# First loads in halves on two queues, filler matmuls on zeros and a re-searched order in a fused sparse-attention and FFN kernel

## The chip, the cores and the metric

One Trainium2 chip, one core of it. The metric is the device time of one execution in microseconds (us). Engines are named as in the profile: PE (TensorE), PEld (its weight loads), DVE (VectorE), ACT (ScalarE), POOL (GpSimd), SP (SyncE); a "q" behind a name, as in SPq or ACTq, is the sequencer of that engine, which issues DMAs.

## What is computed

Two stages in one kernel. The first is attention with 4 batches of 8 heads, 768 positions and head size 64, in which each query keeps six key chunks of 32 positions. The chunks are chosen by an upper bound made of the minimum and the maximum of the keys of a chunk:

```
k_min, k_max = min and max of k over each chunk of 32
ub = sum(max(q*k_min, q*k_max), -1)          # causal over chunks
top_chunks = argsort(ub)[..., -6:]
scores = where(selected and causal, q @ k.T / 8, -1e9)
attn = softmax(scores) @ v
```

The second is a gated FFN over the 3072 rows of 512 values that the attention gives: `xn = x / rms(x) * rms_g`, then `(silu(xn @ w_gate) * (xn @ w_val)) @ w_out` with a hidden size of 1536.

## The kernel before

**Tiling.** Two heads make a pair, so there are 16 pairs, four to a batch. A pair goes through these steps (the names are those of the planner's steps and of the tiles; the lines are those of the kernel before):

- *load* (L486): q and k of the pair, 768 rows, one DMA for each head and tensor into `qnat` and `knat` (192 KB each). The loads of pair 0 put their first head on SP's queue and their second on ACT's; all others are on SP's.
- *turn* (L499): PE transposes, in groups of three 128x128 blocks, two groups for q and two for k; ACT or DVE copies each group out of PSUM (`kt`, `qt`, L315 on ACT and L319 on DVE).
- *kmx, kmn, dif* (L523, L525, L534): maximum, minimum and their difference for each chunk, into `ku`; *relu* (L560): max(q, 0), into `rt`.
- *ub* (L578): 24 matmuls, twelve on `qt` and twelve on `rt`, give the bounds; they are copied out (`ubs`), transposed back (*up*, L602), masked (`ubm`, L610), and twelve MAX8 (L623) find the sixth largest bound of each query; *pick* (L631, L636) makes the selection `selq`, which PE transposes (`st`, L647) and which ACT and DVE put into the lower or upper half of `qs`.
- *sc, exp, av* (L712, L718, L729, L748): per head six groups of scores, an exponential on ACT for each group, and the product with v.

When the four pairs of a batch are through, *norm* scales and transposes the rows (`xs`, `tp`, `xT`) and *ffn* runs on halves of 384 rows: twelve times gate (`gp`, L864), tanh (`sg`, L871), `tg` (L877), value (`vp`, L885), `hh` (L893), then the output product `po` (L905), its copy `osb` and a DMA out.

**What sets the order.** Nothing is reordered by a compiler. Every step is given to `Order.add` with the engines that may run it, an assumed duration, a rank and the steps it depends on. `Order.run` plays these steps forward: whenever an engine is free, it takes the ready step of lowest rank whose buffers are free, and so fixes the engine and the place of each step. The emitted program is that list, and each engine then executes its own part strictly in that order. A rank is the sum of a due time of the pair or FFN half (`TIMES`: a = prepare, l = load, s = scores, n = norm, f = FFN, w = weights) and an offset for the kind of step (`RANK`, one set for batch 0 and one for the rest). The planner doubles the duration of PE steps that start before `COLD` = 10.0 us.

Constants come first: the identity matrix on POOL, zeros in `ku` and `selq` on DVE, `first` on ACT (a one-column Exp, which also brings the activation table in; L354), the mask helpers `e_all` and `cmf` on POOL. `ke0` copies `e_all` into the first key tile on DVE (L391, L392); `ke` does it for the other two by DMA on SP.

A DMA is issued with one of eight completion semaphores of its kind; where one of them is used again, the issuing engine waits until the earlier DMA on it has landed. In the program before, ACT's second load (the second head of k of pair 0) waits in this way for a first load of q.

Of the kernel before, what the change touches and what calls it, by code (L numbers as in the profile page):

```python
# [24 lines left out]

RANK = (
    dict(
        av=-17.99, dif=13.38, eps=15.18, exp=27.56, kC=-0.16, kE=17.53, kT=-23.78, kload=11.87,
        kmn=22.63, kmx=-12.26, max=-61.12, qC=54.11, qE=9.45, qT=-26.18, qload=3.56,
        relu=19.97, root=46.9, sc=-0.2, sel=-44.38, selC=-65.79, selT=-14.62, sq=17.6, tp=7.31,  # L30
        tpE=23.87, ub=-8.14, ubE=18.31, ubm=-7.93, up=-18.76, vload=-10.11, xb=16.97, xs=25.31,
    ),
    dict(
        av=-15.37, dif=-18.4, eps=-17.61, exp=10.72, gate=-5.25, hh=-22.22, kC=13.17, kE=-4.98,
        kT=-1.03, kload=0.17, kmn=-41.84, kmx=7.41, mask=-29.68, max=20.31, out=-9.4, po=2.14,
        poE=-2.1, qC=3.39, qE=-3.84, qT=-9.81, qload=-3.16, relu=-0.35, root=5.16, sc=-14.52,
        sel=-54.35, selC=-24.54, selT=7.81, sq=37.75, tanh=-21.52, tg=-0.17, tp=-45.38,
        tpE=12.9, ub=-13.71, ubE=24.1, ubm=13.82, up=-10.31, val=1.94, vload=19.85, xb=5.4,
        xs=11.14,
    ),  # L40
)

TIMES = dict(
    pace0=1.79, pace1=0.05, pacen=0.06, step=0.1, w=-2.85, w0=-2.54, w1=11.0, w2=43.12,
    w3=21.59,
)
for p, x in enumerate((
    13.52, 22.61, 22.24, 36.48, 50.85, 112.1, 73.87, -93.04, 37.77, 179.84, 214.26, 206.91,
    226.56, 220.49, 246.48, 309.33,
)):  # L50
    TIMES[f"a{p}"] = x
for p, x in enumerate((
    -126.16, -42.1, -31.16, -25.49, -5.8, -2.4, 25.7, 37.05, 124.03, 155.87, 181.98, 170.69,
    131.44, 202.23, 282.06, 292.24,
)):
    TIMES[f"l{p}"] = x
for p, x in enumerate((
    -21.19, 10.14, 25.24, 47.31, 25.73, 45.99, 41.69, 141.19, 75.77, 129.26, 185.37, 166.25,
    277.81, 251.34, 143.95, 194.34,
)):  # L60
    TIMES[f"s{p}.0"] = x
for p, x in enumerate((
    101.79,
), 3):
    TIMES[f"s{p}.3"] = x
for i, x in enumerate((
    -27.88, 91.19, 93.6, 105.43, 90.44, 106.14, 282.0, 341.37,
)):
    TIMES[f"n{i // 2}.{i % 2}"] = x
for i, x in enumerate((  # L70
    50.8, 120.12, 121.42, 191.74, 229.9, 291.93, 266.48, 339.66,
)):
    TIMES[f"f{i // 2}.{i % 2}"] = x
for i, x in enumerate((
    2.53, 0.58, 0.91, 2.16, 0.75, 2.5, 0.51, 0.73,
)):
    TIMES[f"pacef{i // 2}.{i % 2}"] = x

class Buf:
# [138 lines left out]
def kernel(  # L224
# [84 lines left out]
    def pe(n):  # L309
        return 0.003 + n / 2400.0  # L310

    def evict(e, out_, in_, scale=None):
        if e == "ACT":
            if scale is None:
                nc.scalar.activation(out=out_, in_=in_, func=ACT.Copy)  # L315
# [20 lines left out]
    e_all = const.tile([D, S], BF16, name="e_all")  # L336
# [10 lines left out]
    def make_ident(e):  # L347
# [6 lines left out]
    c_act = add("first", "ACT", 1.6, -99, lambda e: nc.scalar.activation(  # L354
        out=first[:], in_=ident_f[:, 0:1], func=ACT.Exp), [c_id])
# [31 lines left out]
    c_ke = [None] * NB  # L387
    for i in range(NB):
        if i == 0:
            c_ke[i] = add("ke0", "DVE", 1.05, -50, lambda e: (  # L390
                nc.vector.tensor_copy(KE[0][0][D:2 * D, :], e_all[:]),  # L391
                nc.vector.tensor_copy(KE[0][1][0:D, :], e_all[:])), [c_e])  # L392
        else:
            c_ke[i] = add("ke", "SP", 1.0, -25, lambda e, i=i: (
                nc.sync.dma_start(out=KE[i][0][D:2 * D, :], in_=e_all[:]),
                nc.sync.dma_start(out=KE[i][1][0:D, :], in_=e_all[:])), [c_e], load=200000)

# [73 lines left out]
    def prep(c, i0, nb, at, lr):  # L471
# [7 lines left out]
        for w, src in (("k", k), ("q", q)):  # L479
            nat[w], big[w] = Buf("nat"), Buf("qt")  # L480

            def load(e, w=w, src=src):
                t = tile_of(nat[w], [P, NT, 2, D], FP32, w + "nat")
                for hl in range(2):
                    eng = nc.scalar if p == 0 and i0 == 0 and hl else nc.sync
                    eng.dma_start(out=t[:, 0:nb, hl, :], in_=src[b, h0 + hl, cols].rearrange(  # L486
                        "(t p) d -> p t d", p=P))

            ld = add(w + "load", "SP", 1.1, rank(lr, b, w + "load"), load, opens=[nat[w]],
                     load=n * 512)  # L490

            evs = []
            for j0 in range(0, nb, 3):
                bank = Buf("ps", "prep")

                def turn(e, w=w, j0=j0, bank=bank):
                    t = tile_of(bank, [P, 3 * P], FP32, "p" + w)
                    for j in range(3):
                        nc.tensor.transpose(  # L499
                            t[:, j * P:(j + 1) * P],  # L500
                            nat[w].tile[:, j0 + j].rearrange("p h d -> p (h d)"), ident_f[:])

                tr = add(w + "T", "PE", 0.33, rank(at, b, w + "T", j0, "step"), turn, [ld, c_id],
                         opens=[bank], uses=[nat[w]])
# [11 lines left out]

        mx = Buf("small")

        def red(e, which):
            view = big["k"].tile[:, 0:n].rearrange("p (c t) -> p c t", t=CH)  # L520
            if which == 0:
                t = tile_of(mx, [P, NCH], FP32, "kmx")
                nc.vector.tensor_reduce(out=t[:, 0:c1 - c0], in_=view, axis=AXX, op=ALU.max)  # L523
            else:
                nc.vector.tensor_reduce(out=KU[c.ku.slot][:, 0, c0:c1], in_=view, axis=AXX,  # L525
                                        op=ALU.min)

        r0 = add("kmx", "DVE", 0.06 + n * 0.00106, rank(at, b, "kmx"), lambda e: red(e, 0), done["k"],
                 opens=[mx], uses=[big["k"]])
        r1 = add("kmn", "DVE", 0.06 + n * 0.00106, rank(at, b, "kmn"), lambda e: red(e, 1),  # L530
                 done["k"] + c_ku, opens=[c.ku], uses=[big["k"]])
# [6 lines left out]
        df = add("dif", "", {"DVE": 0.12, "POOL": 0.2}, rank(at, b, "dif"), diff, [r0, r1],  # L538
                 uses=[mx, c.ku], port=True)
        c.dif[i0] = df  # L540

# [426 lines left out]
```

## Time and profile before

| | |
|---|---|
| device time, median of 3 runs | 328.62 us (328.37 to 329.08) |
| the profiled execution: span from first to last instruction | 461.2 us |
| mean granted TensorE clock in the profiled execution | 0.663 |
| granted clock, first 12 us / from 13 us on | 1.00 / 0.65 |

The profiled execution is the only one with a trace. No total time of its own is given beside the span, and its span is longer than the whole of an unprofiled run, since TensorE had a lower clock in it. Times in the trace's rows are us from the start of the span. A row of the timeline gives the start, the duration, the engine, the line, the operation, out<-in, and how many instructions were merged.

### The profile page before, as it was taken

The numbers are of one execution on the slowest core, as the hardware profiler recorded it, in microseconds if no ns is written. First come the engines' busy times: TensorE is split into PE (matmuls) and PEld (weight loads), VectorE is DVE, ScalarE is ACT, GpSimd is POOL, SyncE is SP. The second block draws the span as 40 slices with busy tenths as digits, with TensorE's granted clock in tenths as the row PEclk, the third lists the DMA queues.
The fourth block names the chain that finished last, engine by engine and source line by source line (L and its number), as shares of the span: only waits on it lengthen the run. The fifth ranks groups of instructions, "written<-read, shape, count | busy, mean of one in ns | idle before, by whom it ended". The sixth has DMA issues, their size and how long they took to land.

```text
span 461.2 us, 7853 instructions
## 1 busy us (share of the span) xinstructions
PE 446.6 (97%) x2978; PEld 253.4 (55%) x2996; DVE 246.5 (53%) x663; ACT 214.3 (46%) x448; POOL 118.0 (26%) x172
## 2 busy tenths in 40 slices
PE   3999999999999999999999999999999999999996
PEld 2677754665666555435666664654565644534442
DVE  2977776665465735404767564367046465603520
ACT  3777772463556643114656684630473634123201
POOL 7755342314442420002552453200110110000000
PEclk9666666666666666666666666666666666666666
DMA  9999769248848250003430203100100000011002
GB/s 186 210 207 143 104 105 100 41 47 53 185 89 134 18 112 9 0 30 105 111 36 1 18 2 46 41 1 1 47 24 0 2 0 1 1 63 52 0 0 91
DMA packets 82645, 27.89 MB, mean 60 GB/s; under 512 B 75568, under 2 KB 79408, under 8 KB 82608
## 3 DMA queue, kind: packets, MB, share of 16 engines
q1 hardware_dynamic: 52528, 19.14, 17.9%
q0 software_dynamic: 28512, 7.87, 17.3%
q10 hardware_dynamic: 1568, 0.39, 0.5%
q8 instruction: 23, 0.38, 0.3%
q14 instruction: 14, 0.11, 0.1%
HBM read 28.57 MB, written 6.29 MB: 76 GB/s over the span
## 4 chain that ended last, share of the span: by engine, by line
PE 96%; DMA 2%; ACT 1%; issue 1%; ACTq 0%
PE vp L885 20%; PE gp L864 20%; PE po L905 20%; PE sc L712 12%; PE av L748 6%; PE ub L578 5%; PE pk L499 3%; PE pq L499 3%; PE tp L830 2%; PE up L602 2%; PE st L647 2%; DMA knat<-in_k_dram 1%; PE sc L718 1%; DMA qnat<-in_q_dram 1%; ACT pt L729 0%
## 5 line engine op out<-in xcount | busy, mean ns | idle before, releaser
L885 PE MATMUL vp<-xT,wv 128*128 128x384 bf16 x384 | 107.5, 430 | 0.0
L864 PE MATMUL gp<-xT,wg 128*128 128x384 bf16 x384 | 107.3, 430 | 0.0
L729 ACT ACTIVATE pt<-sc 128x512 bf16<-128x512 f32 x192 | 91.1, 551 | 20.5 <-PE sc L712 16.6
L905 PE MATMUL po<-wo,hh 128*128 128x512 bf16 x274 | 97.8, 513 | 1.9 <-issue 0.8
L871 ACT ACTIVATE sg<-gp 128x384 bf16<-128x384 f32 x96 | 47.1, 491 | 88.9 <-PE gp L864 78.9
L877 DVE SCALAR_TENSOR_TENSOR tg<-sg,gp 128x384 bf16<-128x384 bf16 x96 | 52.5, 550 | 52.2 <-ACT sg L871 51.4
L893 DVE TENSOR_TENSOR hh<-vp,tg 128x384 bf16<-128x384 f32 x96 | 53.1, 555 | 38.1 <-PE vp L885 37.9
L712 PE MATMUL sc<-qs,ke 89*128 89x128 bf16 (+5 forms) x416 | 72.1, 309 | 0.4 <-PE sc L712 0.2
L885 PEld LDWEIGHTS <-wv 128*128 128x128 bf16 x384 | 45.3, 120 | 43.7 <-issue 3.4
L864 PEld LDWEIGHTS <-wg 128*128 128x128 bf16 x384 | 45.1, 120 | 41.4 <-issue 2.5
L905 PEld LDWEIGHTS <-hh 128*128 128x128 bf16 x288 | 33.5, 120 | 46.8 <-issue 43.8
L735 POOL TENSOR_SCALAR_AFFINE_SELECT pt<-pt 128x512 bf16<-128x512 bf16 (+1 forms) x48 | 24.8, 532 | 102.1 <-ACT pt L729 100.5
L748 PEld LDWEIGHTS <-pt 128*128 128x128 bf16 x672 | 39.1, 111 | 16.5 <-issue 8.2
L712 PEld LDWEIGHTS <-ke 89*128 89x128 bf16 (+1 forms) x420 | 38.2, 116 | 16.0 <-issue 8.6
L748 PE MATMUL av<-vx,pt 128*128 128x65 bf16 x672 | 45.2, 217 | 0.3 <-ACT pt L729 0.2
L317 ACT ACTIVATE osb<-po 128x512 f32<-128x512 f32 x23 | 13.7, 597 | 64.5 <-PE po L905 64.5
L319 POOL CAST ke<-kt 64x768 bf16<-64x768 f32 x31 | 26.1, 843 | 61.0 <-ACT kt L315 57.5
L319 POOL CAST qs<-qt 64x768 bf16<-64x768 f32 x31 | 29.0, 936 | 49.1 <-ACT qt L315 32.5
L499 PE MATMUL pq<-ident_f,qnat 128*128 128x128 f32 x96 | 20.4, 358 | 5.2 <-DMA qnat<-in_q_dram 5.2
L499 PE MATMUL pk<-ident_f,knat 128*128 128x128 f32 x96 | 21.7, 354 | 2.7 <-DMA knat<-in_k_dram 2.5
L525 DVE TENSOR_REDUCE ku<-kt 128x24 f32<-128x768 f32 x16 | 15.1, 945 | 12.7 <-ACT kt L315 12.6
L820 DVE SCALAR_TENSOR_TENSOR xs<-xb,ri,gains 128x512 bf16<-128x512 bf16 x24 | 17.3, 758 | 7.8 <-PE tp L830 5.2
(70 smaller groups left out, 366.7 us busy)
## 6 DMA issues: line engine op xcount, KB each, us to landing
out_dram<-osb SPq DMA_DIRECT2D x24, 256.0 KB, 2.0
qnat<-in_q_dram SPq DMA_DIRECT2D x31, 192.0 KB, 4.8
knat<-in_k_dram SPq DMA_DIRECT2D x31, 192.0 KB, 4.5
vx<-in_v_dram POOLq DMA_DIRECT2D x16, 192.0 KB, 4.7
wv<-in_moe_w_val_dram POOLq DMA_DIRECT2D x2, 768.0 KB, 7.9
wg<-in_moe_w_gate_dram POOLq DMA_DIRECT2D x2, 768.0 KB, 7.0
wo<-in_moe_w_out_dram POOLq DMA_DIRECT2D x2, 768.0 KB, 7.6
ke<-e_all SPq DMA_DIRECT2D x4, 96.0 KB, 3.5
```

The source lines that it names most:

```text
L319: engine[e].tensor_copy(out_, in_)
L499: nc.tensor.transpose(t[:, j * P:(j + 1) * P], nat[w].tile[:, j0 + j].rearrange("p h d -> p (h d)"), ident_f[:])
L712: nc.tensor.matmul(t[:, x:x + m, :].rearrange("p a b -> p (a b)"), ke[kk, kb * P:(kb + 1) * P], qs[kk, q0 * P:(q0 + m) * P], start=not tri ...
L729: nc.scalar.activation(out=t[:, 0:nn, :], in_=sc.tile[:, 0:nn, :], func=ACT.Exp, scale=SCALE)
L735: nc.gpsimd.affine_select(out=pt.tile[:, 0:nd, :], in_=pt.tile[:, 0:nd, :], compare_op=ALU.is_ge, fill=0.0, base=0, pattern=[[0, nd], [1, ...
L748: nc.tensor.matmul(av.tile[:, qi - i0, :], pt.tile[:, x, :], VX[c.v.slot][:, hl * NT + kb, :], start=(begin and m == 0), stop=(left[0] == ...
L864: nc.tensor.matmul(t[:], wg[:, g, hs], XT[b].tile[:, g, cols], start=(g == 0), stop=(g == NP - 1))
L871: nc.scalar.activation(out=t[:], in_=gp.tile[:], func=ACT.Tanh, scale=0.5)
L877: nc.vector.scalar_tensor_tensor(out=t[:], in0=sg.tile[:], scalar=1.0, in1=gp.tile[:], op0=ALU.add, op1=ALU.mult)
L885: nc.tensor.matmul(t[:], wv[:, g, hs], XT[b].tile[:, g, cols], start=(g == 0), stop=(g == NP - 1))
L893: nc.vector.tensor_tensor(out=t[:], in0=vp.tile[:], in1=tg.tile[:], op=ALU.mult)
L905: nc.tensor.matmul(po.tile[:], hhs[ht].tile[:, th * P:(th + 1) * P], wo[:, ht, :], start=(ht == 0), stop=(ht == NHT - 1))
```

## The change

Four things are changed.

1. Pair 0 loads k before q, each tensor in two halves of 384 rows, so eight DMAs of 96 KB in place of four of 192 KB, at ranks -200 to -197, ahead of all other loads. The first head stays on SP's queue, the second on ACT's. Each group of transposes waits for its own half, and pair 0's chunk maxima and minima are taken half by half.
2. `busy`: 48 matmuls of 128x512 on a tile of zeros, at ranks from 1000 up, so that the planner puts one wherever it sees PE free and a PSUM bank open. `COLD` is 4.5 in place of 10.0.
3. `ke0` may now run on ACT or DVE, its rank and that of `ke` are searched, and the assumed duration of `first` is 3.2 in place of 1.6.
4. All numbers of `RANK` and `TIMES` are new.

The core of the diff:

```diff
-    COLD = 10.0
+    COLD = 4.5
...
+    BUSY = 48
...
-    c_act = add("first", "ACT", 1.6, -99, lambda e: nc.scalar.activation(
+    c_act = add("first", "ACT", 3.2, -99, lambda e: nc.scalar.activation(
         out=first[:], in_=ident_f[:, 0:1], func=ACT.Exp), [c_id])
+    zeros = const.tile([P, 4 * P], BF16, name="zeros")
+    c_zero = add("zeros", "DVE", 0.2, -101, lambda e: nc.vector.memset(zeros[:], 0.0))
+
+    def busy(bank):
+        def go(e):
+            t = tile_of(bank, [P, 4 * P], FP32, "busy")
+            nc.tensor.matmul(t[:], zeros[:, 0:P], zeros[:], start=True, stop=True)
+        return go
+
+    for i in range(BUSY):
+        bank = Buf("ps")
+        add("busy", "PE", pe(4 * P), 1000.0 + i, busy(bank), [c_zero], opens=[bank])
...
-            c_ke[i] = add("ke0", "DVE", 1.05, -50, lambda e: (
+            c_ke[i] = add("ke0", "", {"DVE": 1.05, "ACT": 1.4}, {"ke0": 1.0}, lambda e: (
...
                 for hl in range(2):
-                    eng = nc.scalar if p == 0 and i0 == 0 and hl else nc.sync
+                    eng = nc.scalar if p == 0 and hl else nc.sync
...
-            ld = add(w + "load", "SP", 1.1, rank(lr, b, w + "load"), load, opens=[nat[w]],
-                     load=n * 512)
+            if p == 0:
+                ld = [add(w + "load", "SP", 0.55, -200 + 2 * (w == "q") + r0 / 3,
+                          lambda e, load=load, r0=r0: load(e, r0=r0, rn=3), opens=[nat[w]],
+                          load=3 * P * 512) for r0 in range(0, nb, 3)]
...
+        step = 3 if p == 0 else nb
+        for x0 in range(0, nb, step):
+            after = done["k"][x0 // 3:(x0 + step) // 3]
+            lead = {"": -10.0} if p == 0 and x0 == 0 else {}
```

Since the planner decides the places, the diff alone doesn't show the order; the two programs' lists of instructions do. At the start they read as follows.

- ACT, changed: the two halves of k (second head), the table load, `first`, then the two halves of q (second head). The first of these two waits for the completion semaphore of the second half of k, of one head, and the second for that of the other head. Then come two `kt` copies, two copies of `e_all` into `ke`, one cast of `kt`, one `qt` copy and so on.
- SP, changed: the two halves of k, the two of q, both heads of q of pair 1, both heads of k of pair 1 (waiting for the first half of k of pair 0), four `ke` DMAs, q and k of pair 2.
- PE, changed, up to the first scores (n x busy stands for n filler matmuls): 7 x busy, k of pair 0 (two groups of three transposes), 2 x busy, first group of q, 3 x busy, second group of q, 8 x busy, q of pair 1 (six transposes), 4 x busy, ub of pair 0 (24 matmuls), k of pair 1 (six), 1 x busy, up of pair 0 (four), 9 x busy, q of pair 2 (six), 4 x busy, ub of pair 1 (24), 5 x busy, st of pair 0 (six), k of pair 2 (six), up of pair 1 (four), 1 x busy, first scores. The last four busy stand between scores of batch 0.
- PE, before: q of pair 0 (six), k of pair 0 (six), q of pair 1 (six), k of pair 1 (six), ub of pair 0 (24), q of pair 2 (six), up (four), ub of pair 1 (24), q of pair 3 (six), up of pair 1 (four), st of pair 0 (six), k of pair 2 (six), first scores.
- DVE, changed, from the bounds of pair 0 on: `ubs`, `kt` of pair 1, `ubm`, the minimum for pair 1, six MAX8, the maximum for pair 1, six MAX8, relu of pair 2, pick. In the program before, both reductions of pair 1 stand ahead of `ubm` of pair 0, and between `ubm` and pick stand only the difference of pair 1, the twelve MAX8 and the relu of pair 2.
- ACT from the first exponential to the first tanh: 69 instructions before, among them 53 exponentials; 70 after, 48 of them exponentials, with three more `qt` copies, two more squares and one more `xT` copy.
- PE from the first scores to the first gate, and from there to the end: the same set of matmuls in another order, but for the four busy.

More of the change, by code (lines that the diff above doesn't have):

```diff
@@ L27 @@
     dict(
[L28 to L31, printed above, removed]
+        av=-385.99, dif=23.89, eps=127.6, exp=-99.16, kC=-21.51, kE=-195.36, kT=-8.09,
+        kload=36.52, kmn=22.78, kmx=49.34, max=-78.03, qC=32.58, qE=80.5, qT=-0.22, qload=29.48,
@@ L32 @@
+        relu=-7.46, root=336.47, sc=-46.3, sel=61.68, selC=-105.52, selT=-19.85, sq=-160.55,
+        tp=-213.72, tpE=46.81, ub=-184.82, ubE=80.91, ubm=-122.84, up=-120.0, vload=-55.6,
+        xb=6.0, xs=22.85,
     ),
     dict(
-        av=-15.37, dif=-18.4, eps=-17.61, exp=10.72, gate=-5.25, hh=-22.22, kC=13.17, kE=-4.98,
-        kT=-1.03, kload=0.17, kmn=-41.84, kmx=7.41, mask=-29.68, max=20.31, out=-9.4, po=2.14,
-        poE=-2.1, qC=3.39, qE=-3.84, qT=-9.81, qload=-3.16, relu=-0.35, root=5.16, sc=-14.52,
@@ L52 @@
[L52 to L77, printed above, removed]
+        av=-218.73, dif=-87.31, eps=-285.15, exp=-55.93, gate=-8.31, hh=9.81, kC=-136.06,
+        kE=115.43, kT=-64.67, kload=88.45, kmn=-78.89, kmx=32.99, mask=45.94, max=9.98,
+        out=25.68, po=61.14, poE=217.17, qC=97.05, qE=46.47, qT=-24.69, qload=65.23, relu=6.55,
@@ L85 @@
+        root=-321.21, sc=-4.45, sel=23.17, selC=-20.05, selT=-63.82, sq=147.27, tanh=387.07,
+        tg=-65.3, tp=6.28, tpE=-112.86, ub=-27.5, ubE=190.62, ubm=38.34, up=-218.73, val=-0.05,
+        vload=215.91, xb=-88.1, xs=96.87,
+    ),
+)
+TIMES = {
[15 rows of a table added]
+}
 class Buf:
@@ L480, in prep, with load @@
             nat[w], big[w] = Buf("nat"), Buf("qt")
-            def load(e, w=w, src=src):
-                t = tile_of(nat[w], [P, NT, 2, D], FP32, w + "nat")
+            def load(e, w=w, src=src, r0=0, rn=nb):
+                if nat[w].tile is None:
+                    tile_of(nat[w], [P, NT, 2, D], FP32, w + "nat")
+                t = nat[w].tile
                 for hl in range(2):
-                    eng = nc.scalar if p == 0 and i0 == 0 and hl else nc.sync
-                    eng.dma_start(out=t[:, 0:nb, hl, :], in_=src[b, h0 + hl, cols].rearrange(
-                        "(t p) d -> p t d", p=P))
-            ld = add(w + "load", "SP", 1.1, rank(lr, b, w + "load"), load, opens=[nat[w]],
-                     load=n * 512)
+                    eng = nc.scalar if p == 0 and hl else nc.sync
+                    eng.dma_start(out=t[:, r0:r0 + rn, hl, :],
+                                  in_=src[b, h0 + hl, (i0 + r0) * P:(i0 + r0 + rn) * P].rearrange(
+                                      "(t p) d -> p t d", p=P))
+            if p == 0:
+                ld = [add(w + "load", "SP", 0.55, -200 + 2 * (w == "q") + r0 / 3,
+                          lambda e, load=load, r0=r0: load(e, r0=r0, rn=3), opens=[nat[w]],
+                          load=3 * P * 512) for r0 in range(0, nb, 3)]
+            else:
+                ld = [add(w + "load", "SP", 1.1, rank(lr, b, w + "load"), load, opens=[nat[w]],
+                          load=n * 512)] * 2
             evs = []
@@ L517, in prep, with red @@
         mx = Buf("small")
-        def red(e, which):
-            view = big["k"].tile[:, 0:n].rearrange("p (c t) -> p c t", t=CH)
+        def red(e, which, x0, xn):
+            view = big["k"].tile[:, x0 * P:(x0 + xn) * P].rearrange("p (c t) -> p c t", t=CH)
+            a0, a1 = x0 * 4, (x0 + xn) * 4
             if which == 0:
-                t = tile_of(mx, [P, NCH], FP32, "kmx")
-                nc.vector.tensor_reduce(out=t[:, 0:c1 - c0], in_=view, axis=AXX, op=ALU.max)
-            else:
[L525 to L531, printed above, removed]
+                if mx.tile is None:
+                    tile_of(mx, [P, NCH], FP32, "kmx")
+                nc.vector.tensor_reduce(out=mx.tile[:, a0:a1], in_=view, axis=AXX, op=ALU.max)
+            else:
+                nc.vector.tensor_reduce(out=KU[c.ku.slot][:, 0, c0 + a0:c0 + a1], in_=view,
+                                        axis=AXX, op=ALU.min)
+        reds = []
+        step = 3 if p == 0 else nb
+        for x0 in range(0, nb, step):
+            after = done["k"][x0 // 3:(x0 + step) // 3]
+            lead = {"": -10.0} if p == 0 and x0 == 0 else {}
+            reds += [
+                add("kmx", "DVE", 0.06 + step * P * 0.00106, {**rank(at, b, "kmx"), **lead},
+                    lambda e, x0=x0: red(e, 0, x0, step), after, opens=[mx], uses=[big["k"]]),
+                add("kmn", "DVE", 0.06 + step * P * 0.00106, {**rank(at, b, "kmn"), **lead},
+                    lambda e, x0=x0: red(e, 1, x0, step), after + c_ku, opens=[c.ku],
+                    uses=[big["k"]])]
         def diff(e):
@@ L536, in diff @@
                 in1=KU[c.ku.slot][:, 0, c0:c1], op=ALU.subtract)
-        df = add("dif", "", {"DVE": 0.12, "POOL": 0.2}, rank(at, b, "dif"), diff, [r0, r1],
+        df = add("dif", "", {"DVE": 0.12, "POOL": 0.2}, rank(at, b, "dif"), diff, reds,
                  uses=[mx, c.ku], port=True)
```

20 lines of the change are left out of this document (4 added, 16 removed), and 15 rows, old and new, of the table TIMES.

## The prediction

> **What bounds the kernel now.** I read the totals first, then the granted clock, then the stretches before the FFN, and last the timeline of the first 22 us.
>
> ```profile
> span 461.2 us, 7853 instructions
> PE 446.6 (97%) x2978; PEld 253.4 (55%) x2996; DVE 246.5 (53%) x663; ACT 214.3 (46%) x448; POOL 118.0 (26%) x172
> ```
> ```profile
> core 0: 461.2 us, clock 0.663
> ```
>
> PE is busy nearly throughout, but at a granted clock of 0.663. The runs without a trace took 328.62 us, less than this span. PE's 446.6 us at 0.663 are 296 us at full clock; with the 14.6 us in which PE sat idle that is 311 us, and 18 us of the median remain for what lies around the span and for idle time that only a faster PE shows. So the timed runs had about the full clock, at least 296 / 314 = 0.94. I therefore take the profiled execution's own rows, multiply PE's rows from its throttled part by 0.65, leave all other engines and DMAs as they are, and put the difference on the median of 328.62; the throttled execution comes at the end of the second part.
>
> ```profile
> 12.00:13.00 1.00, 1.00 (x7) 0.93 (x5) 1.00 (x2) 1.00 (x4) 0.30 (x1) 0.94 0.61 143
> 13.00:14.00 1.00, 0.91 (x20) 0.26 (x23) 0.97 (x3) 0.77 (x2) 0.93 (x2) 0.65 1.01 233
> 20.00:30.00 10.00, 10.00 (x101) 7.79 (x100) 7.48 (x26) 8.33 (x18) 5.14 (x6) 0.65 1.48 200
> 30.00:40.00 10.00, 10.00 (x134) 6.55 (x131) 6.52 (x25) 6.61 (x15) 5.67 (x8) 0.65 1.57 202
> 40.00:60.00 20.00, 19.69 (x228) 13.90 (x226) 16.74 (x58) 16.15 (x35) 8.55 (x12) 0.65 0.69 107
> ```
>
> The columns are the stretch, its length, the busy time of PE, PEld, DVE, ACT and POOL, the granted clock, the DMA share and GB/s. The clock falls at 13 us. From 20 to 60 us, batch 0's attention, PE is busy 39.7 us, which are 25.8 at full clock; ACT has 31.1 and DVE 30.7. With PE at full speed this stage belongs to ACT and DVE and starts with the first scores. Behind the first gate PE alone carries the time.
>
> ```profile
> 63.33 1.16 PE L864 MATMUL gp<-xT,wg 128*128 128x384 bf16 x4
> ```
>
> From 63.3 us to the end are 398 us, at full clock 260. So the time is: start to first scores, an ACT-bound stage, and a PE-bound stage whose matmuls the change leaves as they are. What the change can do for certain is to shift the first scores.
>
> ```profile
> 0.81 3.79 DMA qnat<-in_q_dram
> 4.62 4.61 DMA knat<-in_k_dram
> ```
> ```profile
> 0.80 0.49 ACTq L486 DMA_DIRECT2D qnat<-in_q_dram  x1
> 2.61 0.20 ACT L354 ACTIVATE first<-ident_f 128x1 f32<-128x1 f32 x1
> 4.62 0.37 ACTq L486 DMA_DIRECT2D knat<-in_k_dram  x1
> 9.27 1.54 PE L499 MATMUL pk<-ident_f,knat 128*128 128x128 f32 x6 [2.54 <-DMA knat<-in_k_dram]
> 11.88 1.36 PE L499 MATMUL pk<-ident_f,knat 128*128 128x128 f32 x6
> 13.33 0.80 PE L578 MATMUL ub<-qt,ku 64*32 64x256 f32 x12
> 13.94 0.84 PE L578 MATMUL ub<-rt,ku 64*32 64x256 f32 x12
> 14.71 1.09 PE L499 MATMUL pq<-ident_f,qnat 128*128 128x128 f32 x6
> 20.76 0.47 PE L712 MATMUL sc<-qs,ke 89*128 89x128 bf16 x4
> ```
>
> The chain of waits (first fence) says what is slow at the start. ACT is through with `first` at 2.81, yet issues its k load at 4.62: it waits for a q load that lands at 4.60. The k load then takes 4.61 us, and everything up to the bounds, which end at 14.78, hangs on it. The first scores follow 6.0 us later.
>
> **The change part by part.** *Loads.* In the changed program ACT issues its halves of k at once, so k comes early. But its halves of q stand behind `first` and wait for the second halves of k, just as k waited for q before.
>
> ```profile
> DMA to landing us min/median/max: 3.2/5.4/5.9
> ```
> ```profile
> 0.80:2.00 1.20, 0.00 (x0) 0.00 (x0) 1.05 (x6) 0.68 (x1) 1.12 (x4) 1.00 0.02 6
> 2.00:3.00 1.00, 0.00 (x0) 0.00 (x0) 0.45 (x2) 0.80 (x2) 0.93 (x5) 1.00 0.99 227
> 8.00:9.00 1.00, 0.00 (x0) 0.00 (x0) 0.00 (x0) 0.13 (x1) 0.99 (x2) 1.00 1.36 217
> ```
>
> The fastest q load took 3.2 us; so the first halves of k land at 0.8 + 3.2 = 4.0, and the second, issued 0.5 us later (0.49 for an issue), at about 4.7. Only then does ACT issue q, at 4.7 and 5.2. The queue of SP is full then as it was before (217 GB/s at 8 us), so ACT's 192 KB take what they took before: 4.6 us from the first issue, the second half at 9.2 and the first about 0.6 us earlier, at 8.6. Between 3.2 us for a half and the row's 4.6 for a whole I take the latter, since both halves share a full queue: 8.4 is the low end for the last half, 9.8 (5.2 + 4.6) the high one. The last load of pair 0 thus lands when it did before (9.23), only it is q and not k. That is a gain, since the reductions on k are then done and q needs a transposition, a copy and a relu.
>
> The Trainium skill speaks against two queues: "DMA: Bandwidth & Descriptors", in its section "Issuing engines are not separate DMA queues", says that DMAs from several engines interleave on the same 16 engines and save issue time only. The trace agrees, with 217 to 227 GB/s whether ACT's queue has a load or not; by it k's 384 KB are there no sooner than 1.7 us after the first bytes at 2.0, about 3.7, and by two full-rate queues they would be at 2.9, which the first seven filler matmuls hide either way.
>
> *Filler matmuls.* The list of the changed program puts twelve of them, and q of pair 1, between q and the bounds of pair 0.
>
> ```profile
> 405.18 10.42 PE po L905 x32
> 58.74 1.44 PE ub L578 x24
> ```
>
> A 128x512 matmul is 0.326 us at 0.65 here, 0.21 at full clock; six fp32 transposes 1.09 us in the row of 14.71 us, 0.71 at full clock, against 1.54 in the first row, cold; `ub` 1.44, 0.94 at full clock. Seven fillers from about 1.1 us on, doubled while cold (1.54 / 0.71 is 2.2), end about when k lands and cost nothing; their cover is the wait for k. They should bring PE to full speed before q lands. Then: first q group 8.6 to 8.96, three fillers to 9.6, second q group to 9.96, eight fillers 1.70 to 11.66, q of pair 1 to 12.37, four fillers 0.85 to 13.2, bounds to 14.15. Without the twelve the bounds would need only `qt` and `rt`:
>
> ```profile
> 15.38 0.95 ACT L315 ACTIVATE qt<-pq 128x384 f32<-128x384 f32 x2
> 13.81 0.55 DVE L560 TENSOR_SCALAR rt<-qt 128x768 f32<-128x768 f32 x1
> ```
>
> that is 9.96 + 0.47 + 0.55 and hand-overs, about 11.2. So 2 us of the gain of 2.6 are spent on fillers, and the bounds of pair 0 end 0.6 us sooner than at 14.78.
>
> *From the bounds to the first scores.* Here the order is worse.
>
> ```profile
> 16.38 0.46 DVE L610 TENSOR_TENSOR ubm<-up,cmf 128x288 f32<-128x288 f32 x1 [0.31 <-PE up L602]
> 14.28 0.94 DVE L523 TENSOR_REDUCE kmx<-kt 128x24 f32<-128x768 f32 x1
> 16.88 0.61 DVE L623 MAX8 m<-ubm 128x8 f32<-128x24 f32 x6
> 18.66 0.46 DVE L631 SCALAR_TENSOR_TENSOR selq<-m,ubm 128x288 bf16<-128x288 f32 x1
> 19.04 0.19 DVE L636 TENSOR_SCALAR selq<-m 128x12 bf16<-128x12 f32 x1
> 15.64 0.63 PE L602 MATMUL up<-ident_f,ubs 96*128 96x96 f32 x4
> 19.28 0.58 PE L647 MATMUL st<-ident_b,selq 128*128 128x128 bf16 x6
> 19.90 0.81 ACT L315 ACTIVATE qs<-st 64x768 bf16<-64x768 bf16 x1 [0.45 <-PE st L647]
> ```
>
> PE: k of pair 1 to 14.86, a filler 15.07, `up` (0.63 x 0.65 = 0.41) 15.5. DVE: `ubm` to 16.05, then pair 1's minimum (0.94) 17.0, six MAX8 17.6, its maximum 18.55, six MAX8 19.2, relu of pair 2, pick (0.65) 20.4. Before, both reductions had run while PE made the bounds of pair 0; now they stand in its chain, 1.9 us. PE meanwhile: nine fillers 17.4, q of pair 2 18.1, four fillers; the bounds of pair 1 wait for the maximum at 18.55 and the difference on POOL, to about 19.9; five fillers 20.95; `st` (0.38) 21.35, though its input is there at 20.4. Then ACT's copy into `qs` to 22.25, and on PE k of pair 2, `up` of pair 1 and a filler (0.71 + 0.41 + 0.21) to 22.7. The first scores come at 22.7, against 20.76 in the row, or 20.3 with `up` and `st` at full clock: 2.4 us later.
>
> *What hides it.* From the first exponential to the first tanh ACT has 53 exponentials and 16 others before, 48 and 22 after.
>
> ```profile
> L729 ACT ACTIVATE pt<-sc 128x512 bf16<-128x512 f32 x192 | 91.1, 551 | 20.5 <-PE sc L712 16.6
> ```
>
> Five exponentials fewer (2.8 us) and six instructions of about 0.5 more come out even, so nothing hides the 2.4 us, and the first gate moves by as much. Four late fillers add 0.85 us at most to the PE-bound part, or nothing in a gap; I take nothing, as the next row to it, 20.5 us in which ACT waited, shows gaps of its kind. `ke0` on ACT (two copies near 0.8 us) ends before q lands; the new ranks behind the first gate are taken as even, with both ends kept for the range. Sum: 328.62 + 2.4 = **331.0 us**.
>
> In an execution throttled to 0.65 as the profiled one, each of the 20 fillers between q and the first scores costs 0.33 and not 0.21, and the twelve ahead of the bounds alone put them off by 1.4 us more: a span of about 465 instead of 461.2.
>
> **The rivals.** *Fillers harmless (same).* If ACT's q were not held and went out right behind `first` at 2.81, its halves would land from 6.1 to 6.6, the bounds end near 11.7 and, by the same steps, scores begin at 20.2: 328.5. Against it stands the row of 4.62. Here the first part of the change does in effect not do what it says, for half of q.
>
> *The search pays later (faster).* Of the 18 us left over above, some is idle PE time behind the first scores at full clock. An order that removes a third of it takes off 6 us and gives 325.0. For it: the stage of batch 0 is bound by ACT and DVE together, where order matters. Against it: PE's idle time in the trace of before is nearly all at the start, and the start of the new order misses its own plan by about 3 us for q.
>
> *PE stays cold (slower still).* The seven early fillers run for some 3 us and then PE waits about 2 us for q. If it runs at the speed of the first row until 12 us, the fifteen fillers from 8.6 us on take 0.46 and not 0.21: 3.7 us more, 334.7. It decides as soon as PE is not at full speed by 8.6 us. The Trainium skill, "TensorE: Matmul & The Clock Gate", section "Part 1: The HAM clock gate", has half clock released after some 3.4 us of sustained work in a free-running window, which leaves it open whether 3 us are enough; the trace agrees in kind, since the six transposes at 11.88 us take 1.36, between the 1.54 at 9.27 and the 1.09 at 14.71. A later order with new gaps in PE would give the same time.
>
> **How the numbers follow.** Later scores and nothing else, 331.0 (330 to 332.5): 0.45. Cold PE or new gaps, about 334.7: 0.13. Same, 328.6: 0.09. Faster by the search, about 325: 0.33. The range leaves out the outer parts of the last case (more than a third of the 18 us recovered) and of the second, about 0.1 each at most: 324.0 to 335.0. About 0.2% (0.66 us) is what a measurement of this kernel can tell from no change. Slower by more 0.57, within 0.10, faster by more 0.33. The likeliest case's own range stands above.
>
> **What would show it.** Right: ACT's q halves issued near 4.7 and 5.2 us; second q group on PE at about 9.2; eight fillers back to back behind it while `qt` and `rt` are ready; bounds of pair 0 ending at 14 or later; both reductions of pair 1 behind `ubm`; first scores at 22 to 23 us, later if throttled. Wrong: q landing before 8 us, the first scores ahead of 20.7, the first tanh not moved although the first exponential did, or PE idle time behind the first gate that differs by some us.

## The result and the profile after

The changed kernel takes 334.0 us (median of 4 runs, 333.5 to 334.35) against 328.63 for the kernel before: ratio 1.0142, interval 1.0113 to 1.017. It is slower by 5.4 us; the forecast was 331.0, slower. The four runs are two of 333.5 and 333.69 us, at a mean granted clock of 0.993 and 0.994, and two of 334.30 and 334.35 at 0.988 and 0.989. The trace is of the run of 333.5, and why the other two had the lower clock is not shown.

The trace of the kernel before shown above was an exception: none of the later traces has a mean granted clock below 0.98. The kernel before was therefore run again for a trace that can be laid beside the other (b_again below). These are the first lines of the page and the clock, of the changed kernel and then of the kernel before, again:

```profile
span 331.8 us, 7954 instructions
PE 320.8 (97%) x3020; PEld 203.8 (61%) x3044; DVE 245.0 (74%) x672; ACT 205.9 (62%) x441; POOL 117.8 (36%) x173
core 0: 331.8 us, clock 0.993
```
```profile
span 328.3 us, 7871 instructions
PE 312.9 (95%) x2996; PEld 201.9 (61%) x2996; DVE 241.9 (74%) x663; ACT 206.2 (63%) x448; POOL 119.2 (36%) x172
core 0: 328.3 us, clock 0.994
```

PE is busier after the change, by 7.9 us, and the kernel is slower: the fillers count as busy. The runs that gave these traces took 333.5 and 330.03 us, so only 1.7 us lie around a span, and the 18 us that the prediction had left over are mostly PE's own time: it is busy for 312.9 us at this clock, and not for 296.

Where the time went is read from two rows of each kernel: the first scores in the timeline, and the first and last gate of the tile `gp` ("56.2 to 309.9" in a gate row are its first and last start). First the kernel before, again:

```profile
20.23 0.38 PE L712 MATMUL sc<-qs,ke 89*128 89x128 bf16 x4 [0.23 <-ACT qs L315]
...
L864 PE MATMUL gp<-xT,wg x384: 323/326/328, 56.2 to 309.9; 128*128 128x384 bf16 x192
```

then the changed one:

```profile
24.98 0.87 PE L720 MATMUL sc<-qs,ke 128*128 128x128 bf16 x5
...
L872 PE MATMUL gp<-xT,wg x384: 323/326/337, 58.9 to 315.7; 128*128 128x384 bf16 x192
```

The first scores are 4.75 us later. From there to the first gate are 36.0 us before and 33.9 after, and from the first gate to the end 272.1 and 272.9. The 36.0 contain about 1.3 us that this execution lost to a fall of PE's clock from 51.5 to 55 us (last section): from the bounds at 51.3 to the first gate it takes 4.96 us, and f1, f2 and f6, three kernels of the same order without this fall (below), take 3.64, 3.63 and 3.64. So it is 34.7 against 33.9. The sum, 4.75 - 0.8 + 0.8 = 4.75, comes within 0.1 us of the difference between 333.5, the run of the changed kernel's trace, and 328.65, an undisturbed run of the kernel before. On balance the loss lies ahead of the first scores.

The chain of waits of the changed kernel there (start, duration, what):

```profile
1.25 3.17 PE busy L341 x7
4.42 1.28 PE pk L498 x6
5.70 0.81 PE busy L341 x2
6.51 2.36 issue
8.87 0.52 PE pq L498 x3
9.39 0.84 PE busy L341 x3
10.23 0.16 issue
10.38 0.88 PE pq L498 x3
11.26 2.71 PE busy L341 x8
13.97 0.66 PE pq L498 x6
14.63 0.86 PE busy L341 x4
15.49 1.01 PE ub L586 x24
16.50 0.80 PE pk L498 x6
...
17.91 1.89 PE busy L341 x8
19.80 0.66 PE pq L498 x6
20.45 0.86 PE busy L341 x4
21.32 1.01 PE ub L586 x24
22.33 1.18 PE busy L341 x5
23.51 0.43 PE st L655 x6
```

Fillers are on the chain nearly all the way: twelve stand between the second group of q (10.38) and the bounds of pair 0 (15.49), and k of pair 1 and the selection's transposes wait behind others. The "issue" of 2.36 us at 6.51 names no releaser; it is read as PE waiting for q, since q's transposes come next and the wait goes when q is loaded sooner (e2 below). The timeline shows why q is late:

```profile
3.19 0.20 ACT L333 ACTIVATE first<-ident_f 128x1 f32<-128x1 f32 x1
4.52 0.98 ACTq L479 DMA_DIRECT2D qnat<-in_q_dram  x2
8.87 0.52 PE L498 MATMUL pq<-ident_f,qnat 128*128 128x128 f32 x3 [2.38 <-issue]
10.38 0.88 PE L498 MATMUL pq<-ident_f,qnat 128*128 128x128 f32 x3 [0.16 <-issue]
```

ACT is through with `first` at 3.39, waits for k until 4.52, and its second half of q is used at 10.38. And PE's clock fell while it waited (windows; the clock is the third number from the end):

```profile
8.00:9.00 1.00, 0.13 (x1) 0.16 (x2) 0.01 (x1) 0.97 (x2) 0.95 (x3) 1.00 1.33 230
9.00:10.00 1.00, 1.00 (x6) 0.41 (x5) 0.00 (x0) 0.50 (x2) 0.86 (x1) 0.86 1.10 240
12.00:13.00 1.00, 1.00 (x4) 0.36 (x3) 0.52 (x1) 0.99 (x2) 0.00 (x0) 0.50 1.98 175
13.00:14.00 1.00, 1.00 (x6) 0.53 (x5) 0.00 (x0) 0.65 (x1) 0.00 (x0) 0.94 1.32 196
```

It is at 0.50 from 9.7 to 13.1 us (worked out from the 0.86 and the 0.94), so that eight fillers take 2.71 us.

The 4.75 us have two parts. The bounds of pair 0 end at 16.50, and in the kernel before, again, at 14.49, as its chain shows:

```profile
12.93 1.56 PE ub L578 x24
```

That is 2.0 us. From there to the first scores the changed kernel takes 8.48 us and the kernel before 5.74: another 2.7, which do not hang on the late q. The kernel without fillers (e1 below) still takes 7.84, so only about 0.6 of them are fillers. In e1's chain both reductions of pair 1 stand between the bounds of pair 0 and the selection, as the prediction had it:

```profile
17.24 0.94 DVE ku L526
18.70 0.85 DVE kmx L524
```

No run took them out of the chain, so that they are the other 2 us is read from the chains alone.

### The profile page after: what moved, and what is told of

Read it like the earlier page. It is cut to its first block, busy times and chain, and to the rows that moved or that the text cites. A ratio compares the mean times of both kernels' runs of the same rounds, so it can differ in the third digit from the quotient of the medians.

```text
span 331.8 us, 7954 instructions
## 1 busy us (share of the span) xinstructions
PE 320.8 (97%) x3020; PEld 203.8 (61%) x3044; DVE 245.0 (74%) x672; ACT 205.9 (62%) x441; POOL 117.8 (36%) x173
## 4 chain that ended last, share of the span: by engine, by line
PE 83%; DVE 6%; ACT 5%; issue 2%; DMA 2%; POOL 1%; ACTq 0%; POOLq 0%
PE gp L872 18%; PE vp L893 17%; PE po L913 16%; PE sc L720 8%; PE av L756 6%; PE ub L586 4%; PE busy L341 4%; PE pq L498 3%; PE pk L498 3%; ACT pt L737 2%; DMA vx<-in_v_dram 2%; PE tp L838 1%; PE st L655 1%; ACT qs L294 1%; PE up L610 1%
## 5 line engine op out<-in xcount | busy, mean ns | idle before, releaser
L737 ACT ACTIVATE pt<-sc 128x512 bf16<-128x512 f32 (+3 forms) x192 | 89.7, 570 | 6.3 <-PE sc L720 5.1
L893 PE MATMUL vp<-xT,wv 128*128 128x384 bf16 x384 | 76.2, 326 | 0.0
L872 PE MATMUL gp<-xT,wg 128*128 128x384 bf16 x384 | 75.6, 326 | 0.0
L913 PE MATMUL po<-wo,hh 128*128 128x512 bf16 x268 | 66.6, 379 | 1.1
L720 PE MATMUL sc<-qs,ke 128*128 128x128 bf16 (+5 forms) x420 | 54.3, 251 | 0.4
L893 PEld LDWEIGHTS <-wv 128*128 128x128 bf16 x384 | 36.3, 98 | 22.3 <-issue 0.4
L720 PEld LDWEIGHTS <-ke 128*128 128x128 bf16 (+1 forms) x420 | 29.7, 97 | 9.9 <-issue 1.2
L296 ACT ACTIVATE osb<-po 128x512 f32<-128x512 f32 x23 | 13.9, 604 | 30.6 <-PE po L913 30.6
L772 DVE TENSOR_TENSOR xb<-av,rden 128x384 bf16<-128x384 f32 (+1 forms) x34 | 18.2, 534 | 1.2
L631 DVE MAX8 m<-ubm 128x8 f32<-128x24 f32 x192 | 18.8, 169 | 0.1
L526 DVE TENSOR_REDUCE ku<-kt 128x24 f32<-128x768 f32 (+1 forms) x17 | 15.3, 898 | 4.2 <-ACT kt L294 4.0
```

Of the source, the lines that this page charges most:

```text
L720: nc.tensor.matmul(t[:, x:x + m, :].rearrange("p a b -> p (a b)"), ke[kk, kb * P:(kb + 1) * P], qs[kk, q0 * P:(q0 + m) * P], start=not tri ...
L737: nc.scalar.activation(out=t[:, 0:nn, :], in_=sc.tile[:, 0:nn, :], func=ACT.Exp, scale=SCALE)
L872: nc.tensor.matmul(t[:], wg[:, g, hs], XT[b].tile[:, g, cols], start=(g == 0), stop=(g == NP - 1))
L893: nc.tensor.matmul(t[:], wv[:, g, hs], XT[b].tile[:, g, cols], start=(g == 0), stop=(g == NP - 1))
L913: nc.tensor.matmul(po.tile[:], hhs[ht].tile[:, th * P:(th + 1) * P], wo[:, ht, :], start=(ht == 0), stop=(ht == NHT - 1))
```

## The experiments

The table has all kernels, with the same two readings from their traces, in us; in those of the new order, from "changed" to e6, only fillers or loads are edited, and f5 has an order of its own. The ratio is that to the kernel before, with its interval.

| kernel | first scores | first gate | scores to gate | gate to end | time | ratio |
|---|---|---|---|---|---|---|
| before, again | 20.23 | 56.2 | 36.0 (34.7) | 272.1 | 330.03, one run | |
| f1: loads on SP | 19.47 | 54.9 | 35.4 | 272.1 | 329.49 | 0.9995 to 1.0039 |
| f2: and early fillers | 17.96 | 54.6 | 36.6 | 272.1 | 329.09 | 0.9984 to 1.0025 |
| f6: and gains later | 18.60 | 54.1 | 35.5 | 272.1 | 327.71 | 0.9926 to 0.9971 |
| h1: delayed bounds | 22.95 | 59.0 | 36.0 (34.7) | 272.1 | 332.81 | 1.0069 to 1.0126 |
| changed | 24.98 | 58.9 | 33.9 | 272.9 | 334.00 | 1.0113 to 1.017 |
| e1: no fillers | 23.12 | 56.9 | 33.8 | 272.3 | 331.18 | 1.0047 to 1.0098 |
| e2: q on SP | 21.09 | 55.0 | 33.9 | 272.9 | 329.62 | 0.9996 to 1.0036 |
| e3: both | 22.31 | 56.3 | 34.0 | 272.4 | 330.33 | 1.0027 to 1.007 |
| f3: gap filled | 23.78 | 57.7 | 33.9 | 272.3 | 331.82 | 1.0056 to 1.0105 |
| f4: q on SP, 24 fillers | 22.12 | 56.1 | 34.0 | 272.4 | 330.23 | 0.9998 to 1.0045 |
| e6: q on SP, gains later | 21.03 | 54.9 | 33.9 | 272.9 | 329.65 | 0.9984 to 1.0026 |
| f5: changed, old ranks | 25.37 | 65.5 | 40.1 | 280.4 | 348.71 | 1.0559 to 1.062 |

In brackets: less 1.3 us for the fall of the clock ahead of the first gate (f1, f2 and f6 have none in their traces). The theories are A, that the late first scores pass to the end one for one, and B, that the new order behind them costs the time.

**b_again.** No edit.

> The kernel before, unchanged, for a trace at the clock of the timed runs. Both theories expect about 328.6 us. Theory A (the late first scores pass to the end one for one) expects the first scores near 20.5 us and as long a stretch from there to the end, within 1 us, as the 306.8 us of the changed kernel (331.8 less 25.0). Theory B (the new order behind the first scores costs the time) expects that stretch to be 304 us or less here.

The stretch from the first scores to the end is 308.1 us, 1.3 longer than the 306.8 of the changed kernel and so 0.3 outside what A expected; without the 1.3 us of the fall of the clock the two are equal. B expected 304 or less, and that is refuted.

**e1_no_fill.**

```diff
-            nc.tensor.matmul(t[:], zeros[:, 0:P], zeros[:], start=True, stop=True)
-        return go
+        return lambda e: None
```

> The changed kernel with its planned order kept instruction by instruction, but none of the 48 matmuls on zeros emitted; nothing else is left out. Theory A: the second group of q goes at 10.35 us as before, the bounds of pair 0 no longer wait for twelve fillers and end about 2.5 us sooner than 16.5, the fourteen and five fillers further on are gone too (0.8 us at the point where they held up the selection's transposes), so the first scores come near 21.7 us and the time near 330.7 us. If the fillers bring PE to full speed early enough to pay for themselves, the time stays at 334 or rises. Theory B: 334.0 within 0.7.

331.18: 2.8 us less than the changed kernel, its first scores 1.9 sooner. The fillers cost more than they give here. The bounds end at 15.3 and not at 14, since PE, without them, is at half speed: q of pair 1 takes 1.54 us and not 0.82, and the bounds themselves 1.88 and not 1.01.

**e2_q_sp.**

```diff
-                    eng = nc.scalar if p == 0 and hl else nc.sync
+                    eng = nc.scalar if p == 0 and hl and w == "k" else nc.sync
```

> The changed kernel with the second head of q of pair 0 issued on SP's queue and not on ACT's, so that it doesn't wait for k to land; order and fillers as in the changed kernel. Theory A: q is there near 7 us in place of 10.3, but the twelve fillers, at half speed, still stand ahead of the bounds, which end near 14.6 us in place of 16.5: the time is 332. If the wait of the q load is the whole of the loss, the first scores move by 3.3 us and the time is 330.7. Theory B: 334.0 within 0.7.

329.62, with the first scores 3.9 us sooner: taking away the wait of one queue brings back 4.4 of the 5.4 us. It is more than expected of A, because PE now had no gap, its clock stayed at 1.00, and the same eight fillers took 1.73 us. That wait is still not the whole cause. The bounds of pair 0 now end at 12.50, 2.0 us sooner than in the kernel before, and yet the first scores come 0.9 later, since the way from there takes 8.59 us and not 5.74: the early q pays for the longer way behind it.

**e3_both.** The edits of e1 and e2.

> Both edits: no fillers emitted, and q of pair 0 on SP's queue. Theory A: bounds of pair 0 end near 11.5 us, and the first scores come near 19.5 to 20.5 us, since pair 1's reductions still stand in the chain: the time is 328.5 to 329.5. Theory B: above 332.

330.33, and the expectation was too good: with q in time the fillers earn their place. Without them PE finds nothing to do from 13.9 to 16.0 us, while it waits for q of pair 2, and its clock is at half from 16.9 to 23.75 us. The windows of e3:

```profile
14.00:15.00 1.00, 0.00 (x0) 0.00 (x0) 1.00 (x3) 0.00 (x0) 0.83 (x1) 1.00 1.36 240
15.00:16.00 1.00, 0.03 (x1) 0.06 (x1) 1.00 (x8) 0.00 (x0) 0.82 (x1) 1.00 1.19 254
17.00:18.00 1.00, 1.00 (x24) 0.43 (x12) 0.73 (x4) 0.40 (x2) 0.51 (x2) 0.50 1.04 187
23.00:24.00 1.00, 1.00 (x9) 0.45 (x7) 1.00 (x3) 0.91 (x2) 0.94 (x2) 0.62 2.09 155
```

**f1_before_sp.** The kernel before with `eng = nc.sync` for all loads.

> The kernel before, order and ranks unchanged, with all four loads of pair 0 (q, then k) issued on SP's queue, so that the second head of k no longer waits for a q load. Theory A (first scores pass to the end one for one): k lands near 6.8 us in place of 8.8, the first scores come 2 us sooner, near 18.2, and the time is 326.6 us. Rival: another load or the mask takes the place of k as the last to arrive, or the stage of batch 0 takes the lead up: 328.7 within 0.5.

No change that can be told (329.49). k is there 2.1 us sooner, at 6.71 in place of 8.83, but the first scores come only 0.8 us sooner and the first gate not at all: 54.9, as 56.2 less the 1.3 of the fall. The rival holds.

**f2_before_sp_fill.** f1, and nine fillers ahead of PE's first transposes:

```diff
+    for i in range(9):
+        bank = Buf("ps")
+        add("busy", "PE", pe(4 * P), -1000.0 + i, busy(bank), [c_zero], opens=[bank])
```

> The kernel before with all four loads of pair 0 on SP and nine matmuls on zeros ahead of PE's first transposes, none later. They end near 5.1 us, about when q lands, so PE works without a gap from 1.25 us on. Theory A: PE is at full speed from about 8 us in place of 13, which takes some 1.5 us off the transposes and bounds behind it: first scores near 17 us, time 325.2. If fillers cost what they take, or the clock is not released: 326.6 or more.

The first scores come 2.3 us sooner, at 17.96, and the time is the same (329.09; the runs with a mean clock of 0.997 or more have a median of 328.6, as have those of the kernel before beside them). A falls for an early start. The chain of waits of f2 names what takes the lead away:

```profile
16.73 7.51 DMA qnat<-in_q_dram
24.24 0.14 issue
24.38 0.53 PE pq L511 x3
```

q of a later pair lands at 24.24, and PE's transposes of it start at 24.38, when they started at 24.60 in the kernel before without waiting; PE stood idle for it for 1.60 us. From 20 to 26 us the queue moves 193 to 198 GB/s, and 188 to 205 in the kernel before, again: an early PE did not make it faster.

**f3_bridge.** Five more fillers behind the ninth:

```diff
+            for _ in range(6 if n == 8 else 1):
+                nc.tensor.matmul(t[:], zeros[:, 0:P], zeros[:], start=True, stop=True)
```

> The changed kernel with five more matmuls on zeros in the gap between k and q of pair 0 (6.5 to 8.9 us), order and all else kept. If the gap is what put the clock back to half from 9.3 to 13.0 us, the clock stays, the eight fillers take 1.7 us in place of 2.9, the first scores come 1.3 to 1.5 us sooner and the time is 332.6. If the fall of the clock has nothing to do with the gap, or another wait ends last: 334.0 within 0.5.

331.82, that is 2.2 us less for more work on PE, of which 1.2 are in the first scores. With the gap partly filled the clock stays, and the eight fillers take 1.73 us. The windows of f3:

```profile
9.00:10.00 1.00, 1.00 (x6) 0.41 (x5) 0.00 (x0) 0.55 (x2) 0.84 (x1) 1.00 1.11 227
12.00:13.00 1.00, 1.00 (x8) 0.69 (x7) 0.31 (x1) 0.99 (x2) 0.00 (x0) 1.00 1.99 178
```

**f5_old_ranks.** The changed kernel with the old `RANK` and `TIMES`, and ke0=-50, ke=-25.

> The changed kernel with the numbers of the kernel before in all ranks and due times (the key-tile copies at -50 and -25): new loads, fillers and planner settings without the new search. The planner puts the same fillers ahead of the bounds and 23 ahead of the selection's transposes. Theory A: the start is as late as in the changed kernel, first scores at 24 to 26 us, and the time is 333 to 336. Theory B (the new ranks cost the time): 330 or less.

348.71. The start is as late as expected, but the stage of batch 0 takes 40.1 us and the rest 280.4. B is refuted: with the new loads, fillers and halves the old numbers cost 14.7 us more than the searched ones. Which of these parts they fail on was not followed up.

**f4_q_sp_24.** e2, with the fillers from the 25th on left out.

> The changed kernel with q of pair 0 on SP's queue and only the first 24 of the 48 matmuls on zeros emitted, those up to the bounds of pair 0; order kept. Theory A, now that first scores to first gate took 33.9 us in four kernels of this order: PE stays at full speed without the later fillers, the first scores come up to 0.8 us sooner than the 21.1 of the kernel with all fillers, and the time is 328.8 to 329.6. If PE falls back to half speed in the gaps, as it did with no fillers at all: 330.3 or more.

330.23, and the first scores at 22.12, a microsecond later than with all 48 fillers (329.62; the intervals overlap). In its trace PE's clock was at 0.50 from 16.7 us, behind a gap of 2.5 us, as in e3. The later fillers thus hold the clock there, but what that is worth in time lies within the noise.

**h1_before_late.** The kernel before, with a delay of the bounds alone:

```diff
+            for _ in range(24 if p == 0 else 0):
+                nc.tensor.matmul(t[0][:], zeros[:, 0:P], zeros[:, 0:2 * P], start=True, stop=True)
```

> The kernel before with 24 matmuls of 128x256 on zeros put directly ahead of the bounds of pair 0, nothing else changed: a late start alone, in the old order. They take 2.6 us at full speed, up to 5.1 at half speed. Theory A: the first scores come later by what they take, about 23.5 us, and the time rises by as much, to about 331.7. Rival, after the two kernels whose earlier start gained nothing: the old order's stage of batch 0 is set by its loads, so that a delay up to 2 or 3 us costs less than half of itself: 329.5 or less.

The first scores are 2.7 us later and the time is 4.1 us above the kernel before. The latter mixes runs with and without the fall of the clock. Trace against trace, both with it, the span is 2.8 us longer; its one run at a mean clock of 1.00, 330.88, is 2.2 above the median of such runs of the kernel before beside it, 328.7. In the old order too a late start passes on nearly in full; the rival falls. Start and end are thus not tied alike in both directions: in the old order, with its loads as they are, scores before 20 us gained nothing, and later ones cost about all of their delay.

**f6_gains_late** and **e6_gains_late.** f2 and e2, with the DMA of the gains issued behind the q load of pair 5:

```diff
+                if p == 5 and w == "q":
+                    load_gains()
```

> The old order with pair 0's loads on SP and nine early matmuls on zeros, and the 256 KB load of the gains moved behind the q load of pair 5, out of the queue ahead of pair 2's and pair 3's loads. If the loads are what took the early start away there (q of pair 3 landed at 24.2 us, and PE waited 1.6 us for it), it lands about 1.1 us sooner (256 KB at some 220 GB/s), the first gate comes near 53.5 us in place of 54.6, and the time is near 328 us, below the kernel before. If ACT and DVE set the stage of batch 0: no change, 329.1 within 0.5.

> The changed kernel with q of pair 0 on SP's queue and the load of the gains moved in the same way. Its first scores come at 21.1 us and its first gate 33.9 later, without a wait of PE for a q or k load after 16 us, so the theory that its start sets its time expects 329.6 within 0.5, and a load-bound stage 328.5.

f6 takes 327.71, ratio 0.9949 (0.9926 to 0.9971): it beats both kernels. In its trace q of that later pair lands at 23.93 in place of 24.24 and the first gate comes 0.5 us sooner, less than the 1.1 expected. The medians differ by 1.4 from f2; the run of the trace, 327.88, is the slowest of the seven with a mean clock of 0.997 or more, whose median is 327.0, so the one trace can't show what the others gain. e6 stays at 329.65, as the theory has it in which its start sets its time.

## Why the prediction was right, and where its sizes were off

The direction and the mechanism were right: a later start, put off by the held q, by fillers and by pair 1's reductions, that nothing hides. 334.0 is inside the range; the forecast was 3.0 us short, and the time lies outside the 330 to 332.5 of its likeliest case. By its steps:

- *The bound.* Start, a stage whose length the start doesn't change, and a PE-bound stage: right for a later start. In the seven kernels of the new order the first gate follows the first scores by 33.8 to 34.0 us, while these move from 21.0 to 25.0. The PE-bound part was mis-sized, 272 us and not 260, so PE's time did not follow the clock in full, but it hardly differs between the two kernels (0.8). And "the clock falls at 13 us" misreads the column: PE was at half speed until then (last section). The sums are not hurt, since they take the first rows as cold.
- *Loads.* ACT's q was forecast to be issued at 4.7 and went at 4.52. The second half was forecast at 9.2 with a high end of 9.8, and was used at 10.38. Two halves did not cost what one whole load had cost: where 4.6 us were taken, a half took up to 5.3 us to land, as the loads of q in the first 12 us of the changed kernel show. The sentence that the GB/s are the same with a load on ACT's queue and without rests on two windows that both have one; f2, with all loads on SP, has 217 to 219 GB/s from 6 to 10 us and bears it out.

```profile
DMA to landing us min/median/max: 3.0/3.9/5.3
```

- *Fillers ahead of the bounds.* This is the term that was mis-sized. "They should bring PE to full speed before q lands" was true for a moment only: the first q group and two fillers ran at full speed, then the clock went back to half, and the eight fillers took 2.71 us and not 1.70, the second q group 0.88 and not 0.36. That the wait for q did it is shown by f3, which fills part of it and keeps the clock; with 331.8 us it is 0.8 from the forecast. The rival that PE stays cold, 0.13 and 334.7 us, is nearest in time, but by luck: PE was at full speed when q came and lost it again, and the half speed cost 1.5 us ahead of the bounds, not the rival's 3.7. Its last sentence, on new gaps in PE, comes nearer to what happened.
- *From the bounds to the first scores.* 8.55 us forecast, 8.48 measured (16.50 to 24.98). This is the larger part of the loss, and the prediction had it right, the sum with some luck: the selection was ready 6.9 us after the bounds and not 6.25, since its last steps on DVE took longer, and the fillers ahead of `st` held it for 0.1 us and not for 0.95.
- *What hides it.* Nothing, as forecast: the stage of batch 0 is only 0.8 us shorter.
- *Sum.* Forecast 2.4 us later scores (22.7 against 20.3); measured 4.75 (24.98 against 20.23). The difference, 2.35, comes from the bounds, which ended at 16.50 and not 14.15: 0.8 from the later second half of q (10.38 against a start at 9.6), 1.5 from the half-speed transposes and fillers.
- *The rivals.* With q not held (e2) the first scores came at 21.1 and not the 20.2 of the rival, and the time was 329.6 and not 328.5, within the interval of no change all the same. The search did not pay behind the first gate, 272.9 against 272.1. The case for it, at 0.33, took part of the 18 us left over for idle PE time behind the first scores; the kernel before, again, has 7.3 us of that, 4.9 of them behind the first gate, so the 6 us off were hardly there to be had. The search did pay in another sense, which was not foreseen: without it the new structure costs 348.7.

## What to carry to other kernels

Fillers whose places are fixed beforehand are worth what the loads make of them. Here they cost 2.8 us where q came late (changed against e1), as they stood behind it and ran in part at half speed, and they gave 0.7 where q came early and a later wait would have put the clock back (e2 against e3). Before a load is called the first of all, look at which semaphore it reuses: here the choice of the queue for one load was worth 4.4 us. And an early start and a late start are two different questions; look for the next transfer on the chain before counting a lead as a gain. Nor does a repair that brings the time back show that it took away the only loss: e2 is level with the kernel before, with 2 us won at one place and nearly 3 lost at the next.

## What the runs showed of the hardware

The clock column reads 1.00 from the start of a trace, also where PE is slow: in the changed kernel seven fillers take 3.17 us there, 0.45 each, and in f3 later eight take 1.73, 0.22 each. In the kernel before, again, six transposes of q take 1.51 us at 4.77 and 0.88 at 14.42. So PE starts at about half speed, and a 1.00 ahead of the first change of the clock says nothing of it; nor does a mean clock count that time.

After an idle or half-idle stretch PE's clock falls to 0.50 for 3.4 us or twice that: from 9.7 to 13.1 us in the changed kernel, from 16.9 to 23.75 in e3. "TensorE: Matmul & The Clock Gate" of the Trainium skill, section "Part 1: The HAM clock gate", has a free-running window of about 3.4 us; the traces agree, in that the falls have this length or its double. The section puts the fall behind an idle window of that length; here less was enough: PE was idle for 2.4 us and busy for 1.0 of the 3.4 ahead of the fall in the changed kernel. What share is enough is not shown: f2 had PE busy for 1.9 us from 6.3 to 9.7 and no fall. In the kernel before, again, with PE busy 1.8 of the 3 us ahead, such a fall stood here:

```profile
48.00:49.00 1.00, 0.72 (x10) 0.34 (x8) 1.00 (x8) 1.00 (x4) 0.00 (x0) 1.00 0.83 132
49.00:50.00 1.00, 0.51 (x6) 0.34 (x6) 0.86 (x4) 1.00 (x4) 0.12 (x1) 1.00 1.16 203
50.00:51.00 1.00, 0.60 (x8) 0.35 (x8) 0.97 (x2) 0.99 (x3) 1.00 (x3) 1.00 1.14 206
51.00:52.00 1.00, 0.96 (x22) 0.64 (x28) 0.93 (x4) 0.79 (x2) 0.76 (x1) 0.78 1.08 194
52.00:53.00 1.00, 1.00 (x19) 0.19 (x8) 1.00 (x2) 0.39 (x2) 0.00 (x0) 0.50 0.83 55
54.00:55.00 1.00, 1.00 (x9) 0.77 (x8) 0.22 (x2) 1.00 (x3) 0.25 (x1) 0.52 1.10 186
```

The runs of the kernel before that stand beside the experiments fall in two groups: 27 with a mean granted clock of 0.994 took 329.85 to 331.25 us, 50 with 0.997 or more 328.32 to 329.44. Only one of the 27 has a trace, in which the fall cost 1.3 us, twice what a measurement of this kernel can tell from no change; the medians of the groups are 2.0 apart, and the rest is not explained.
